# Another static order for the steps of an attention and MoE kernel on one core

## The chip, the cores and the metric

The kernel runs on one NeuronCore of one Trainium2 chip. The metric is the device time of one execution in microseconds. The kernel before took 953.86, 952.43 and 950.26 us in three runs, median 952.43.

## The reference

Attention over a batch of 8, with 8 heads, 576 positions and 64 dimensions, is followed by a root mean square norm and a gated feed-forward layer:

```
scores = scale * q @ k.T                       # [8, 8, 576, 576]
mask_local   = (rel >= 0) & (rel < 32)         # heads 0 to 3
mask_strided = (rel >= 0) & (pos_k % 32 == pos_q % 32)   # heads 4 to 7
attn = exp(scores - max) / (sum + 1e-9)
x = (attn @ v)  as [4608 tokens, 512]
xn = x / sqrt(mean(x * x) + 1e-6) * rms_g
out = (silu(xn @ w_gate) * (xn @ w_val)) @ w_out      # 512 -> 1536 -> 512
```

Everything is float32. Both masks leave at most 32 positions to a query, so only small blocks of the scores are computed.

## The kernel before

**Attention.** There are 32 iterations, one for each batch entry and pair of heads. In each, TensorE multiplies blocks of queries and keys into the PSUM tile `pair` (L288, 72 or 80 small matmuls). VectorE scales and masks them (L308, into the tile `pT` or `pp`) and takes the largest of each row (L311). ScalarE does ten exponentials with sums (L315). VectorE forms the reciprocal of the sums (L319, L320), POOL or VectorE multiplies by it (L322), VectorE transposes (L324). Then TensorE multiplies by the values (L300, in two halves that use the same PSUM tile), and ScalarE (L358) or VectorE (L360) copies each half out into `raw`. Squares (L400, L416, L418) and their sums (L421, tile `ssq`) follow for the norm.

**Norm and feed-forward layer.** The 4608 tokens are nine chunks of 512. For chunk 1, a matmul with ones (L430) sums the squares over the partitions, ScalarE takes the root (L480), VectorE makes reciprocals of it (L483) and scales (L487). Each float32 product is three matmuls of rounded parts, high by high, low by high and high by low: `xh` and `xl` (L501, L516), `hh` and `hl` (L598 or L600, L607), and the two halves of each weight tile. The 1536 inner columns are twelve slices of 128. A slice has g (L540, PSUM tile `g`), v (L540, `v`), the gate (L553 tanh on ScalarE, L555, L591 and L584 on VectorE) and four groups of output matmuls (L616, tiles `acc`). L550 adds a correction to g. Chunk 0 is done in this plain form. Chunks 1 and 2 and later chunks save products by sums of blocks: the sums of the weights are formed by VectorE, POOL and ScalarE (L667, L671, L755, L761), stored in DRAM (`tg`, L769) and loaded again (L777). Chunks 3 to 6 are done in pairs (products at L1593, sums at L1624 and L1643, outputs at L1392), the last two as one pair (L1004). Weights that were moved out come back by DMA (L1246, `wg<-wsg`, `wv<-wsv`). The weights arrive packed and are unpacked by VectorE, ScalarE and POOL in the first part (L1736 to L1758).

**What sets the order.** The program first records 3612 steps, each with the engines that may do it, and issues none. The table `ORDER`, text of compressed bytes, then says for each place which of the steps still left comes next and on which of its engines (`Plan.order`, L143):

```
code = zlib.decompress(base64.b85decode(ORDER))
left, out = list(range(n)), []
for k in range(n):
    i = left.pop(code[k] + 256 * code[n + k])
    out.append(self.ops[i][0][ENGINES[code[2 * n + k]]][2])
```

The steps are issued in that order (L1837 to L1839), each engine keeps its own part of it, and waits between engines follow from the data and the reuse of tiles. Nothing is reordered later: a step that waits holds all that stand behind it on its engine. SP's queue holds the DMA issues in the same manner.

Of the kernel before, what the change touches and what calls it, by code (L numbers as in the profile page):

```python
# [20 lines left out]
NB, NH, S, D = 8, 8, 576, 64  # L21
DM, DF = 512, 1536
# [3 lines left out]
P = 128  # L26
KC = DM // P
# [29 lines left out]

ENGINES = ("PE", "DVE", "ACT", "Pool", "SP")
ORDER = (
    "c-rk)*OMH_dG9o#dve^J4Y#+uw|jeg8MvHr;2i=90z@K600v2bVni$^!ID4_06`KAkSt23#9&g1v?$BvDqD6*a@p3KQ@LDz@W0_FKj_6h-7|Y&`PmPyy1BiX*`DsNzy5"  # L60
    "u{@7Ld~AL)UiXr^Oo8bAc&$1uj4rny+NHRUDs@C!!{tCugcOFmQ2JM?~A(f2C*73HL&>&}ykb4)QFIbxh%dB}M5sAU_<11HS;*)c<b`wqB!k9hj#^nUXD@!ezpg*JY#j"
    "^YUej|?xElNQ6%tvNcxaA#+GP<QLYxVDV{qh|O06P~mGUFo<}sNHYc&6;z>w9P|9R<-}PR`OR?sraiMzu1xdyt&(IH2%)&>;LVK`hH#e*{6R^`aY?C{0|@hec>bWw;wi"
    "t)BME`{^sY+4^}>J?*8RZ<Mlsp#((zG7hlGo|LIu#)6e^V^3hL>=`W4X9-r4f-mlN%AD5@~Pd{lTANe0P*M8uPdmn#)?4zakzlU!j^!^Qew>4qC6Ww_`vff+{t#22t_u"
    "hWjzw`DVqV^jfhI?QCz;eIewBB!DxBh7H+TFzu?oQk9IAP(~IVZjwIPac&?3p{)&yKzkIuD+?{hD`cz`3#ft>t}QG5p46zqc6&2d+fH3+opzAM*C0^9P<q&pdJIig)qS"
    "9`F45<>%w2C!SyTo{hZc=EJj3Cg+yU&OY||;;eW2^r3TKJGF4&@h4Qbc4qQ)_Y~@jE<5$%XOCYPKK4{=*OQ?;Jm!Y0?&<qGr@Ch!?JPbKtj1?nrcd`xo%Bw$qK6-8MfD"
    "?%qtOvRG5W`g2W$I_2m1E?<KDi#d-tri@X>0s_)vdsSJ5r3EG0{e@q({bc6+1I=&~12E`$>c-Dqq&o-PhXlkGwjkKT>nYb4$Ju4E;-y_DQqyg7U0vm3L?$Jb|Go%vysB"
    "!BFet^)6sA_{`&?dVSY*2(zs+i`H>ruFb^?)B@zzrI?&Rt~;-xD+I>Kbzc4E*?nSYghb|o_Ob9DLUbcaag<(6~fpHLigE<>vIS_FZRPTqOJHyP&ncG$J}J`uv@q}A3fR"
    "^MHRPj#E;#A?~O$6xD}Y2gH1NH-e@>hX?ZzXau%Hv3&DKFIa;1^$|cXVCmh?dsd-;$?AW!-n44T-Y{^}`<1SdvoafA#&Xi;C9GRS4wucwGCDxfqSg}?#s_Vv>!B$2>)?"
# [36 lines left out]

# [1794 lines left out]
```

## Time and profile before

| | before |
|---|---|
| median of three runs | 952.43 us |
| profiled execution, its own time | 952.13 us |
| its span | 950.0 us |
| mean granted clock of TensorE | 0.977 |
| TensorE (PE), matmuls | 911.8 us busy, 96%, 8708 |
| VectorE (DVE) | 746.8 us, 79% |
| ScalarE (ACT) | 460.2 us, 48% |
| GpSimd (POOL) | 250.1 us, 26% |
| DMA | 220.76 MB, 232 GB/s |

All times are of the one profiled execution, from the start of its span. A row of a timeline gives the start of an instruction or of a few alike, their length, engine and line, the output and input tiles and, in brackets, how long the engine had stood idle before and what ended that. "issue" there means that the profile shows nothing the engine waited for. The granted clock is a share of TensorE's full clock.

### The profile page before, as it was taken

How to read it: one execution, taken by the hardware profiler on the slowest of the kernel's cores; microseconds unless marked ns; L12 is line 12 of the kernel's file. 1: busy time of each engine (PE TensorE's matmuls, PEld its weight loads, DVE VectorE, ACT ScalarE, POOL GpSimd, SP SyncE). 2: the span in 40 equal slices, each digit the busy share in tenths (PEclk: the TensorE clock that was granted, in tenths of full speed). 3: DMA queues.
4: the chain of work that ended last, by engine and by line, in shares of the span. 5: the costliest groups of instructions: out<-in, count | busy, mean ns of one | idle time of the engine just before them, and what ended most of it. 6: DMA issues, size and time to landing. Idle time of an engine off the chain costs nothing.

```text
span 950.0 us, 21761 instructions
## 1 busy us (share of the span) xinstructions
PE 911.8 (96%) x8708; PEld 734.8 (77%) x8708; DVE 746.8 (79%) x1235; ACT 460.2 (48%) x1308; POOL 250.1 (26%) x213
## 2 busy tenths in 40 slices
PE   4899996999999999999999999999999999999998
PEld 3677774787887877886888887888887878888886
DVE  6889997978788899887669999653679896447883
ACT  7779754445333556544444485342336623224330
POOL 2222233233433521444214313200051320014211
PEclk6799997999999999999999999999999999999999
DMA  9865677684666697874763697755655795576462
GB/s 331 320 255 206 202 254 242 242 293 149 233 214 231 223 290 262 304 279 189 255 221 129 212 306 242 294 210 178 246 204 162 223 352 202 204 269 233 122 223 87
DMA packets 95092, 220.76 MB, mean 232 GB/s; under 512 B 9616, under 2 KB 28688, under 8 KB 94992
## 3 DMA queue, kind: packets, MB, share of 16 engines
q1 hardware_dynamic: 94560, 218.83, 66.4%
q8 instruction: 68, 1.11, 0.5%
q10 hardware_dynamic: 432, 0.56, 0.2%
q14 instruction: 32, 0.26, 0.1%
HBM read 172.17 MB, written 47.19 MB: 231 GB/s over the span
## 4 chain that ended last, share of the span: by engine, by line
PE 77%; DVE 10%; DMA 6%; ACT 3%; issue 2%; SPq 1%; DVEq 0%; ACTq 0%
PE acc L1593 10%; PE acc L540 7%; PE v L1593 7%; PE g L1593 6%; PE acc L1392 6%; PE g L540 5%; PE v L1392 4%; PE v L540 4%; PE g L1392 4%; PE v L1004 3%; PE acc L1004 3%; PE g L1004 3%; PE pair L288 2%; DMA wg<-wsg 2%; PE pair L300 2%
## 5 line engine op out<-in xcount | busy, mean ns | idle before, releaser
L540 PE MATMUL g<-xh,wg 128*128 128x512 f32 x184 | 60.3, 410 | 2.8 <-DVE e L555 2.0
L315 ACT ACTIVATE pT<-pT,mx 128x64 f32<-128x64 f32 x160 | 53.4, 336 | 18.5 <-DVE mx L311 18.5
L540 PE MATMUL v<-xh,wv 128*128 128x512 f32 x184 | 57.9, 396 | 0.5 <-DVE or L584 0.5
L315 ACT ACTIVATE pp<-pp,mx 128x64 f32<-128x64 f32 x160 | 53.4, 338 | 10.1 <-DVE mx L311 10.0
L288 PEld LDWEIGHTS pair<-xx,xx 64*32 64x32 f32 (+1 forms) x2432 | 28.0, 109 | 24.8 <-issue 16.0
L288 PE MATMUL pair<-xx,xx 64*32 64x64 f32 (+1 forms) x2432 | 34.3, 234 | 12.6 <-issue 7.2
L540 PEld LDWEIGHTS g<-xh,wg 128*128 128x128 f32 x184 | 35.7, 198 | 13.0 <-DVE e L555 2.9
L540 PEld LDWEIGHTS v<-xh,wv 128*128 128x128 f32 x184 | 33.6, 188 | 7.8 <-DVE or L584 0.6
L540 PE MATMUL g<-xl,wg 128*128 128x512 f32 x92 | 37.1, 403 | 0.0
L358 ACT COPY raw<-pair 128x128 f32<-128x128 f32 (+8 forms) x64 | 20.9, 373 | 32.8 <-PE pair L300 32.7
L671 POOL TENSOR_TENSOR tt<-tt 128x256 f32<-128x256 f32 (+1 forms) x26 | 24.2, 937 | 46.2 <-DVE tt L671 29.2
L540 PE MATMUL v<-xl,wv 128*128 128x512 f32 x92 | 35.9, 391 | 0.0
L540 PE MATMUL acc<-xh,wg 128*128 128x512 f32 x104 | 33.9, 408 | 0.0
L540 PE MATMUL acc<-xh,wv 128*128 128x512 f32 x104 | 33.4, 404 | 0.0
L616 PE MATMUL acc<-or,hh 128*128 128x512 f32 x96 | 30.7, 398 | 0.8 <-DVE or L1758 0.8
L315 ACT ACTIVATION_READ_ACCUMULATOR pp<-pp,mx 128x1 f32 x160 | 30.4, 190 | 0.0
L315 ACT ACTIVATION_READ_ACCUMULATOR pT<-pT,mx 128x1 f32 x160 | 30.1, 188 | 0.0
L553 ACT ACTIVATE e<-g 128x512 f32<-128x512 f32 x23 | 13.7, 598 | 32.6 <-PE g L540 20.0
L1611 ACT ACTIVATE or<-g 128x512 f32<-128x512 f32 x24 | 14.3, 596 | 31.3 <-PE g L1593 27.2
L1593 PE MATMUL acc<-wg,wv 128*128 128x512 f32 x102 | 29.2, 394 | 0.0
L1593 PE MATMUL acc<-wv,wv 128*128 128x512 f32 x102 | 28.7, 390 | 0.0
L1648 POOL TENSOR_TENSOR wv<-or,or 128x512 f32<-128x512 f32 x2 | 2.6, 1291 | 95.6 <-DVE or L1624 95.6
(854 smaller groups left out, 2920.9 us busy)
## 6 DMA issues: line engine op xcount, KB each, us to landing
wv<-wsv SPq DMA_DIRECT2D x36, 512.0 KB, 6.9
wg<-wsg SPq DMA_DIRECT2D x26, 512.0 KB, 7.5
or<-tg SPq DMA_DIRECT2D x22, 512.0 KB, 5.5
th<-tg SPq DMA_DIRECT2D x21, 512.0 KB, 5.9
tl<-tg SPq DMA_DIRECT2D x21, 512.0 KB, 6.0
xx<-in_qT_dram SPq DMA_DIRECT2D x32, 288.0 KB, 5.4
xx<-in_kT_dram SPq DMA_DIRECT2D x31, 288.0 KB, 5.3
wg<-wos SPq DMA_DIRECT2D x32, 256.0 KB, 5.2
```

The source lines that it names most:

```text
L288: nc.tensor.matmul(out=pair_[32 * y:32 * y + m, h, 64 * g:64 * g + 64], lhsT=q[r, PAD + a:PAD + a + m], rhs=k[r, a:a + 64], start=True, st ...
L300: nc.tensor.matmul(out=dst[z // 2][64 * h:64 * h + 64, z % 2, 320 + c:320 + f], lhsT=v[r, 6 * h + j], rhs=t[r, a:a + f - c], start=j == fi ...
L315: nc.scalar.activation(out=tv[:, g], in_=tv[:, g], func=AF.Exp, bias=m[:, g:g + 1], accum_out=z[:, g:g + 1])
L358: nc.scalar.copy(out=d, in_=s)
L540: nc.tensor.matmul(out=out, lhsT=wt[:, w, sl], rhs=xhl[x, kc], start=(n == 0 and i == 0), stop=(n == KC - 1 and i == 2))
L553: op("ACT", act(CH, True), 0, lambda: nc.scalar.activation(out=e(), in_=out, func=AF.Tanh, scale=0.5), reads=[bk], writes=[ek], tab="exp")
L616: nc.tensor.matmul(out=acc[t], lhsT=x[h][:, sl], rhs=wt[:, w], start=(u == 0 and i == 0), stop=(u == NU - 1 and i == 2))
L671: elementwise(width, lambda e: both(e).tensor_tensor(out=dst(), in0=a(), in1=b(), op=ALU.subtract), [], keys)
L1004: nc.tensor.matmul(out=banks[bk], lhsT=w, rhs=X[a, k].tile(y), start=start and k == 0 and i == 0, stop=stop and k == 1 and i == 2, skip_gr ...
L1392: nc.tensor.matmul(out=banks[bks[j]], lhsT=w.tile(v, k, j), rhs=x.tile(k, y), start=start and n == 0 and i == 0, stop=stop and n == KT - 1 ...
L1593: nc.tensor.matmul(out=banks[bk], lhsT=w, rhs=xtile(a, k, y), start=start and k == 0 and i == 0, stop=stop and k == 1 and i == 2, skip_gro ...
L1611: op("ACT", act(CH, True), 0, lambda: nc.scalar.activation(out=temp(dst), in_=banks[bk], func=AF.Copy, scale=scale), reads=bank_keys(bk), ...
```

## The change

The kernel's steps, their number and what each may run on are the same. Only the table `ORDER` is another, and it is one source line longer, so that every line of the changed kernel behind it has a number one higher than in the kernel before. One line of the 48 and its like:

```diff
 ORDER = (
-    "c-rk)*OMH_dG9o#dve^J4Y#+uw|jeg8MvHr;2i=90z@K600v2bVni$^!ID4_06`KAkSt23#9&g1v?$BvDqD6*a@p3KQ@LDz@W0_FKj_6h-7|Y&`PmPyy1BiX*`DsNzy5"
+    "c-rk)*>fDnd7nP#zILuXXD{q777OCO2m%B_kRU*c6iMjdO@fqY5)7?_vTQ37C0nu%$C50`vJ#a;>ONvwNja`c;#BN%Ra}+#yre2m`3q8c$wQvf(>=4G-t&?wG<GqVp6;"
...
```

The steps of the five engines before and after, as counted from the two tables:

| | TensorE | VectorE | ScalarE | POOL | SP |
|---|---|---|---|---|---|
| before | 1007 | 1180 | 646 | 209 | 570 |
| after | 1007 | 1163 | 656 | 216 | 570 |

In the rows below, the number behind a tile's name and the underscore is a serial number; `pT1`, `hl0` and the like are the tiles, and x12 counts matmuls in a row.

TensorE, about 142 to 155 us of the trace before. Above, from left to right of the flow, stand the last products of v, the two halves of the values product (L300) of one attention iteration, the scores (L288) of a later one, and the sum of squares of chunk 1 (L430). In the kernel before:

```order
L540 MATMUL v_68<-xh1_780,wv10_1506 128x512 x2
L540 MATMUL v_68<-xl1_786,wv10_1506 128x512
L540 MATMUL v_68<-xh3_790,wv10_1506 128x512 x2
L540 MATMUL v_68<-xl3_797,wv10_1506 128x512
L300 MATMUL pair_72<-pT1_98,vt1_86 64x64 x12
L300 MATMUL pair_72<-pT1_98,vt1_86 64x48 x4
L300 MATMUL pair_72<-pT1_98,vt1_86 64x16 x4
L300 MATMUL pair_72<-pT1_98,vt1_86 64x64 x12
L300 MATMUL pair_72<-pT1_98,vt1_86 64x48 x4
L300 MATMUL pair_72<-pT1_98,vt1_86 64x16 x4
L288 MATMUL pair_72<-xx2_82,xx1_81 32x64 x36
L430 MATMUL g_67<-ssq_101,ones_64 128x512
L540 MATMUL g_67<-xh0_442,wg10_1520 128x512 x2
```

And the same part of the changed kernel:

```order
L301 MATMUL pair_72<-pT1_98,vt1_86 64x64 x12
L301 MATMUL pair_72<-pT1_98,vt1_86 64x48 x4
L301 MATMUL pair_72<-pT1_98,vt1_86 64x16 x4
L541 MATMUL v_68<-xh1_690,wv10_1475 128x512 x2
L541 MATMUL v_68<-xl1_772,wv10_1475 128x512
L301 MATMUL pair_72<-pT1_98,vt1_86 64x64 x12
L301 MATMUL pair_72<-pT1_98,vt1_86 64x48 x4
L301 MATMUL pair_72<-pT1_98,vt1_86 64x16 x4
L541 MATMUL v_68<-xh3_762,wv10_1475 128x512 x2
L541 MATMUL v_68<-xl3_777,wv10_1475 128x512
L289 MATMUL pair_72<-xx2_82,xx1_81 32x64 x36
L431 MATMUL g_67<-ssq_101,ones_64 128x512
L289 MATMUL pair_72<-xx0_80,xx3_83 32x64 x32
```

One group of v now stands between the two halves of L300 and one between the second half and L288; behind L430 come the scores of the next iteration, where g stood.

VectorE in the same stretch, from the masking of that iteration's scores (L308, into `pT1`) to their transposition (L324). In the kernel before:

```order
L308 SCALAR_TENSOR_TENSOR pT1_98<-pair_72,cb_63 128x640
L311 TENSOR_REDUCE mx1_74<-pT1_98 128x10
L671 TENSOR_TENSOR tt_105<-tt_105 128x256 x2
L755 CAST th0_1792<-tt_105 128x512
L761 TENSOR_TENSOR tl0_1796<-tt_105,th0_1792 128x512
L755 CAST th0_1792<-tt_105 128x512
L761 TENSOR_TENSOR tl0_1796<-tt_105,th0_1792 128x512
L319 TENSOR_SCALAR mx1_74<-su1_76 128x10
L320 RECIPROCAL mx1_74<-mx1_74 128x10
L322 TENSOR_TENSOR pT1_98<-pT1_98,mx1_74 128x640
L324 STREAM_TRANSPOSE pT1_98<-pT1_98 128x640
```

And in the changed kernel:

```order
L309 SCALAR_TENSOR_TENSOR pT1_98<-pair_72,cb_63 128x640
L312 TENSOR_REDUCE mx1_74<-pT1_98 128x10
L556 SCALAR_TENSOR_TENSOR e_100<-e_100,g_67 128x512
L592 SCALAR_TENSOR_TENSOR e_100<-e_100,v_68 128x512
L601 CAST hh0_103<-e_100 128x512
L608 TENSOR_TENSOR hl0_882<-e_100,hh0_103 128x512
L1752 SCALAR_TENSOR_TENSOR th0_106<-or1_1551 128x512
L320 TENSOR_SCALAR mx1_74<-su1_76 128x10
L321 RECIPROCAL mx1_74<-mx1_74 128x10
L323 TENSOR_TENSOR pT1_98<-pT1_98,mx1_74 128x640
L325 STREAM_TRANSPOSE pT1_98<-pT1_98 128x640
```

The weight sums (L671, L755, L761) have left the place between L311 and L319, and the gate and its rounding (L555, L591, L600, L607) stand there.

VectorE at about 431 to 438 us, in the first pair of chunks that is done together: `wv9` and `wv10` are weight tiles that come back by DMA, `or` takes a sum that TensorE needs. In the kernel before:

```order
L1617 TENSOR_TENSOR acc3_71<-acc3_71,e_4810 128x512
L667 TENSOR_TENSOR hl0_4891<-wv10_5076 128x512
L308 SCALAR_TENSOR_TENSOR pT0_97<-pair_72,cb_63 128x640
L311 TENSOR_REDUCE mx0_73<-pT0_97 128x10
L1624 SCALAR_TENSOR_TENSOR or2_4784<-or2_4784,g_67 128x512
L671 TENSOR_TENSOR hl0_4891<-hl0_4891 128x256
L319 TENSOR_SCALAR mx1_74<-su1_76 128x10
L320 RECIPROCAL mx1_74<-mx1_74 128x10
L1624 SCALAR_TENSOR_TENSOR or4_4840<-or4_4840,acc3_71 128x512
```

And in the changed kernel:

```order
L1618 TENSOR_TENSOR acc2_70<-acc2_70,or2_4806 128x512
L668 TENSOR_TENSOR hl0_4872<-wv9_4558 128x512
L672 TENSOR_TENSOR hh0_4883<-hl0_4872,hh0_4883 128x512
L672 TENSOR_TENSOR hl0_4872<-hl0_4872 128x256
L672 TENSOR_TENSOR hl0_4872<-hl0_4872,hh0_4883 128x256
L309 SCALAR_TENSOR_TENSOR pT0_97<-pair_72,cb_63 128x640
L312 TENSOR_REDUCE mx0_73<-pT0_97 128x10
L1625 SCALAR_TENSOR_TENSOR or3_4828<-or3_4828,acc2_70 128x512
```

The L667 that reads `wv10` has left VectorE for POOL, and one that reads `wv9` stands a few places ahead of L308.

## Rows read from the trace of the kernel before

**Rows 1.** Stretches: from:to, us, busy PE PEld DVE ACT POOL, clock, DMA, GB/s
```profile
0.00:50.00 50.00, 32.79 (x778) 25.44 (x779) 37.51 (x74) 37.13 (x127) 11.37 (x24) 0.70 0.88 330
50.00:134.00 84.00, 82.44 (x735) 65.44 (x733) 79.29 (x127) 67.25 (x162) 22.85 (x16) 1.00 0.68 236
134.00:165.00 31.00, 21.80 (x373) 15.76 (x363) 23.62 (x39) 14.08 (x53) 11.27 (x11) 0.78 0.60 199
165.00:340.00 175.00, 172.16 (x1951) 139.00 (x1950) 146.52 (x242) 78.46 (x266) 63.05 (x53) 1.00 0.66 230
...
766.00:950.00 184.00, 179.23 (x787) 147.02 (x785) 120.05 (x198) 52.52 (x93) 26.90 (x20) 1.00 0.59 208
```

**Rows 2.** Page: busy time by engine; a DMA queue (packets, MB, share)
```profile
PE 911.8 (96%) x8708; PEld 734.8 (77%) x8708; DVE 746.8 (79%) x1235; ACT 460.2 (48%) x1308; POOL 250.1 (26%) x213
...
q8 instruction: 68, 1.11, 0.5%
```

**Rows 3.** TensorE's timeline, 134 to 165 us: start, length, instruction, [idle <-releaser]
```profile
134.66 1.02 PE L288 MATMUL pair<-xx,xx 64*32 64x64 f32 x80 [0.55 <-ACT raw L358]
...
137.32 0.50 PE L616 MATMUL acc<-or,hl 128*128 128x512 f32 x1 [0.98 <-DVE hl L607]
...
139.04 0.62 PE L616 MATMUL acc<-or,hh 128*128 128x512 f32 x2
...
139.72 0.62 PE L540 MATMUL v<-xh,wv 128*128 128x512 f32 x2
...
144.67 1.00 PE L300 MATMUL pair<-pT,vt 32*64 32x64 f32 x40 [2.06 <-DVE pT L324]
...
148.47 1.08 PE L288 MATMUL pair<-xx,xx 64*32 64x64 f32 x52 [0.78 <-ACT raw L358]
151.66 0.64 PE L288 MATMUL pair<-xx,xx 64*32 64x64 f32 x20 [2.11 <-issue]
...
155.08 1.22 PE L540 MATMUL g<-xh,wg 128*128 128x512 f32 x2 [0.78 <-ACT srt L480]
...
156.53 1.05 PE L540 MATMUL g<-xh,wg 128*128 128x512 f32 x2
...
157.81 1.05 PE L540 MATMUL g<-xh,wg 128*128 128x512 f32 x2
```

**Rows 4.** VectorE's timeline, 130 to 180 us
```profile
135.50 1.77 DVE L607 TENSOR_TENSOR hl<-e,hh 128x512 fp32r<-128x512 f32 x1
...
142.35 0.17 DVE L319 TENSOR_SCALAR mx<-su 128x10 f32<-128x10 f32 x1 [0.51 <-ACT pT L315]
...
143.67 0.84 DVE L324 STREAM_TRANSPOSE pT<-pT 128x640 f32<-128x640 f32 x1
...
165.92 0.68 DVE L607 TENSOR_TENSOR hl<-e,hh 128x512 fp32r<-128x512 f32 x1
...
175.92 1.20 DVE L319 TENSOR_SCALAR mx<-su 128x10 f32<-128x10 f32 x1
```

**Rows 5.** POOL's timeline, 130 to 180 us
```profile
135.21 1.51 POOL L1758 TENSOR_TENSOR or<-th,or 128x512 fp32r<-128x512 f32 x1 [3.29 <-ACT or L1756]
...
175.79 1.29 POOL L667 TENSOR_TENSOR tt<-wv 128x512 f32<-128x512 f32 x1
```

**Rows 6.** TensorE's timeline of the opening
```profile
15.05 0.44 PE L288 MATMUL pair<-xx,xx 64*32 64x64 f32 x7 [2.80 <-issue]
```

**Rows 7.** TensorE's timeline around 307 us
```profile
307.58 0.50 PE L540 MATMUL acc<-xl,wv 128*128 128x512 f32 x1 [0.70 <-issue]
```

**Rows 8.** VectorE's timeline around 434 us
```profile
433.72 0.69 DVE L667 TENSOR_TENSOR hl<-wv 128x512 f32<-128x512 f32 x1 [1.61 <-DMA wv<-wsv]
```

**Rows 9.** TensorE's timeline around 437 us
```profile
436.65 0.96 PE L1593 MATMUL g<-wg,wg 128*128 128x512 f32 x3 [1.16 <-DVE or L1624]
...
438.96 0.96 PE L1593 MATMUL acc<-wg,or 128*128 128x512 f32 x3 [0.66 <-DVE or L1624]
```

**Rows 10.** TensorE's timeline where the last pair of chunks begins
```profile
773.99 1.63 PE L1004 MATMUL g<-raw,wg 128*128 128x512 f32 x6 [0.98 <-DMA wg<-wsg]
```

More of the change, by code (lines that the diff above doesn't have):

```diff
@@ new lines @@
+    ")|<M;i(Z-89i%*isgv8)ma(M^Pr1QpqVvL!$8w7l_@d`o{)&S_Y+EwV+{WwQDxA<9|BK22m|8W^6mG^`-19zWuqRoAI=7_C|(WR$L;)%`X^OK|mn_AW{Ke*(o_QvTbep"
+    "fdkoRvF;fGV)+gzBgJn^V7r8znSe=9}NqpRT$b+H1$qk6zygi<$miF^uLRP-&Ovp5&gOz=}Xn{uVX#<YWVBw??3-t^jZ9mCG_#%7eD%A>7R=q4E*74`1?CXBmWf~s6}7"
+    "C_j%R-`qSa~Z+c&S?SJ_d{Nk^=Uv)qGq5?np1h#+qE3frSuW;vFVf@pN3m?M|-zt6--Pv_FxAfug`{XYl?veMPy+ORUXOF*Sy%E1|HQ#x6_3d{mZ~fq>-`nfHKD7UCP@"
+    "Dh7t2KA{&wcm3oB8uM^0x=ye87J5bS|`CyD|X$AC;f9Px!C;_N%wgymbFdFP=s($K{uf<Q{r9eDImj+E^=CPx%{99fXg62L$W>V~;N1eB}D%wcOH^k3C^M9$HtXgB#Yh"
@@ new lines @@
+    "r5oScTDrRX#;J4Pau%*^E;yGi4mjtpHqTAD-j&UXP48mi!dT&)+xT|==84?!mUn%{+vtvUgTc$*@Md)6e6+GYG`AT&JaFm4z=cjcefG@s>8R1E)E}rkI6QD-{lp=Ec<5"
+    "*?t{*Pf4j(@BFKe|!>;77}u^8@OsMMF2Dof49%4#*7Z^d)frMMB-N6O*u>IaRxv)#sY<Ne8A<Gu0mcgI&6W6Q1m<&}D~zEr5!_7rL#6=$l?m*eNke=$*c=9&0P{LbaK<"
+    "M7h+w{ZC5QmN6%7f)@~tU`SI)OTa&nacP5@^{PeccKa{8pWuPFWrc?2BSg{MnMz?`JkLH6{GyATEOl%!qUkTN5bIPnPB;6!M-Ti$S<A<gZsm3GdL0i>-nKlaIn~k+J)9"
+    "q=jh%}cX6R}XiujQY=xcWMz{om=0Xt92aR2oN<NsJjDqoFVSX$e*&VDYemghS8VtsPZ;#A--f%IPE_jnK=b~}h9gTu^*mH-5+-@-IcKlA;t(M$kuIv^o6}w!>H)FeAA!"
@@ new lines @@
+    "e!KkCe+!X{g`~792Cm=R)(4RW-e)HCVP<?m!qf+`3hBs+Mil>*f94V99f2Gb%XNtP#djwrLq-=Co}Y4P$)FG^!osR?uMC(TjG`F4)C<C10`ilBIi^=IXw7)9z?JN9$^X"
+    "ksg}Wi&wSS(8@Vo>ps+VhBdpbSp!B(8_<r`o6W}I0ne@0t1r2W?!+rKGB&5pub1LO>g;+^T`8ysj8Sd*di$E%>dm)QbwHVJH_rtV4P2A&yHAegU2>%>kFbl@8j`!({K0"
+    "tz&s%fUsLi7)iYH?-?vzJIX3KaQPnGb*_#_@<Kcjer{p`Z{A9|Q{0fJQsTa_AYRI9L>FXhW{vT%0-j#JouPY&Mgcs<zd5;*-^=uG~{Y^(m8fiXDR9fALD$L)UwL!b;gA"
+    "2i#bR0MOkK%-U%G3Zp<Z&Fa|{h8eEwl_hiRnC=2!$o=b!3ep>az*%5!FSiZo38(M&h2!54u>9jc?jkP9ROPAC*~&V+Gx!%M`9PKLu#1`Ujy-<#5cgxg?%yz!cq{)c@Rv"
@@ new lines @@
+    "{TycUH?%$xq4u>4ObJRX=udW|$k#*=FTs~;7cxDb8i^gIdSo)m4jvgvc>JWNhH3#;&d!Ji10JVUo%Er8^lk3yYEZI`6a!DO6kpdnhrxnr-N^qzs7ch;EVjWlZ9ayq77#"
+    "hBhbj6cHXHvCanVwax7uBipx5^{>^Sh8&FSNbm-Fy#4Ik_nx_7(fkN^F<#b+sTX6cGZ7#)bmHDHqHTTXywbj((5~$)J6301Ph5V6(Aj&RJ;H2%f|ys*-V{?;;uk3S5=l"
+    "+^<}Cl@5Oq0_#&B#2!H986Cht_2JJIC_6IzDJ5hW;U2+**u=&UG1TVkv)WAMS*`qi9pZxO|7}t66h+a?iq|ZnPEJ?!5Xxm$@v%$;Onk#7map52>1d8^SQgPEo!lncvxL"
+    "fo(x=TL9j9ZF{uBww6aLn(ed4LgZ?@<)gHmwGK<Hv!lhG##X&46x#VF?!myn!I{MU%-yi5#IGZ)Qx&vRrzBkK3^24zN254ey9@Fu#B?Ja|$Q#Gz^UN$coT2)oyFUnAc1"
@@ L103 @@
+    "oP8B$7HPbp(yPMP-<QemM$9Lko8j1sWqd?6trG3#qmXT!9jrObx<ZMn#cEWMInkkbQiVK{t525wg_0l5sFJnxx&m|`)*5J>wWNjyv2fHW5YpOn&024|p669uMN78IERR"
+    "*-R;HiASsVtGbjo>PME)9wz4R~Ug1u}r+%h)yx>8naE=OAE|+ljjYBqRUESj#BCt4oI>$Yb&6X@kvT2+YQ7$kmGItHj+R_Uj6PCZ^I#toFq)Xr^QU8npFbfxU79a+bW1"
+    "lri{=|;vvEP|LG?=&XpIF%=!3#0p=m_O#"
 )
```

66 lines of the change are left out of this document (24 added, 42 removed).

## The prediction

> **What bounds the kernel now.** I read the table of stretches first [rows 1]. TensorE is busy in 911.8 of 950.0 us [rows 2], and the reader is to see where the missing 38.2 us lie: 17.2 in the first 50 us, 1.6 from 50 to 134, 9.2 from 134 to 165, 2.8 to 340, 4.8 in the last 184, and the 2.6 that are left from 340 to 766. No other engine has so much work: VectorE stands highest from 50 to 134, with 79.29 of 84 us. So the same instructions in another order can win the idle time of TensorE and no more, apart from the clock: the granted clock is 1.00 in every stretch but two, 0.70 in the first and 0.78 in the third. [...] A triple of 128x512 matmuls takes 0.68 us from start to start at the upper level (139.04 to 139.72) and 1.28 at the lower (156.53 to 157.81) [rows 3].
>
> The second view is TensorE's timeline from 134 to 165 [rows 3], the third VectorE's there [rows 4]. The reader is to see one chain: VectorE's L607 takes 1.77 us at 135.50 instead of the 0.68 of the same line at 165.92 while POOL works on L1758 [rows 4, 5]; TensorE waits 0.98 us for it; the softmax behind it on VectorE starts late, and the values product L300 waits 2.06 us for the transposition L324, the next scores L288 wait 0.78 for a copy out of PSUM, then 2.11 for nothing that the profile shows ("issue"), and the g matmuls wait 0.78 for the root L480. Together 5.73 us of holes that follow one another, after a first one of 0.98.
>
> The fourth view is the waits on "issue". In the opening there are four, the first of 2.80 us [rows 6]. Counted over TensorE's matmuls, weight loads and semaphore rows from the start, the instruction at which TensorE resumes is number 449, 705, 961 and 1473 of them, then 3521 at 151.66 and 7105 at 307.58 [rows 3, 7]: each 256 apart or a multiple of it. The page's queue of instructions moves 68 packets of 1.11 MB together, 16.3 KB each, for 17416 matmuls and weight loads, 256 for a packet [rows 2]. I read this so: TensorE's instructions come in pieces of 256, and a piece of dense small matmuls (L288, L300) is used up before the next has come. A piece can only be made longer in time by what else stands in it.
>
> **The change part by part.** The 3612 steps stay; TensorE's stand 3.3 places away from before on average, 381 steps change their engine (123 from VectorE to POOL, 116 back, 75 from VectorE to ScalarE, 65 back, 2 between ScalarE and POOL).
>
> *134 to 165 us.* The scores before that wait of 2.06 us (L288 at 134.66) now stand four to five groups earlier, and behind them stand ten triples of 0.68 us instead of eight before L300 needs the transposition: 6.8 us of cover for 5.4. Before, the chain from the end of the scores (134.66 + 1.02 = 135.68) to that of the transposition (143.67 + 0.84 = 144.51) took 8.8 us, of which the first 1.5 was VectorE still busy with L607, to 137.27. Without that it is 7.3, so of the 2.06 about 0.5 stays: -1.5. If VectorE is as late as before, it is 8.8 - 6.8 = 2.0 and nothing is won; if it is earlier, -2.06. One triple now stands between the two halves of L300 and one between L300 and L288: 0.68 us each against the wait for a copy, 0.78 at 148.47 and as much, near enough, between the two halves: -1.3. The piece border still lies in the same L288, but its piece now holds those triples, two more less one that left: the TensorE work in it (its instructions in the new order, by their spacing before) rises from 2.8 to 4.0 us, and the 2.11 falls by the same 1.2 to 0.9: -1.2. L430 has a full L288 of 80 matmuls behind it where g stood: about 1.0 us, more than the 0.78 wait for the root: -0.8. The 0.98 for L607 goes too, but its steps are mixed with others in the new order, and I count 0.2 of it. Sum -5.0, bounds 0 and -8 (all the holes named, and the clock held: 3 triples at 1.28 instead of 0.68 are 1.8 more).
>
> *307.58 us.* The piece whose end stalled 0.70 us held 5.2 us of work, counted in the same way, and now holds 9.2: -0.7, bounds 0 and -0.7.
>
> *433 to 439 us.* VectorE stands at L667 until a weight load lands (idle 1.61), behind it wait L308, L311 and L1624, and TensorE waits 1.16 and 0.66 us for two L1624 [rows 8, 9]. The load is now 12 places earlier in SP's queue, and that L667 is on POOL, so that VectorE's queue no longer waits with it: -1.8. Bounds 0 (another L667, with an earlier load, now stands a little ahead of the same place) and -1.8.
>
> *First 50 us.* Border stalls of the same kind stay: the first pieces hold 1.6, 1.6, 1.6, 3.7 and 3.8 us of TensorE's work where they held 1.6, 1.6, 2.5, 4.4 and 3.5. A four-copy evacuation moves from ScalarE and one L1758 from POOL to VectorE. I take 0; bounds -2.8 and +2.8 (one stall as the first of [rows 6] less or more).
>
> *The rest.* What is idle elsewhere is 1.6 + 2.1 + 1.2 us (50 to 134; 165 to 340 without 307.58; the last stretch without what lies behind its last matmul), and 0.8 of the 2.6 later. The largest is the 0.98 at 773.99, for a weight load [rows 10]. The pair that begins there now needs two loads at its first product, queued one behind the other at once: between none and twice the 0.98, I take it as unchanged. Of the others I count 1.5 as gone. Against it stand new ones: in an order in which TensorE's steps move by three places, waits of the size of those there now come up elsewhere, above all from 50 to 134, where VectorE has 4.7 us to spare; I take +2.5, bounds 0 and +5.
>
> Sum: -5.0 - 0.7 - 1.8 + 0 - 1.5 + 2.5 = -6.5 us. From the profiled execution's 952.13 that is 945.6; the median of the runs is 952.43, 0.3 above it, so 945.9 for what will be timed.
>
> **The rivals.**
>
> *The gain of 134 to 165 is eaten by VectorE and POOL.* For it: beside POOL's instructions VectorE's own take longer. L319, 0.17 us at 142.35 with POOL idle, took 1.20 at 175.92 while POOL had L667, and L607 its 1.77 beside L1758 [rows 4, 5]: 1.0 and 1.1 us too long. The change gives POOL seven steps more, and puts four L671 and one L1758 on POOL just there. Four such collisions at 1.0 us in the chain L607, L319, L322 and the sums of squares behind it are 4 us: -2.5 in all instead of -6.5, thus 949.9. Against it: VectorE's column shrinks by 17 steps, at 0.6 us (746.8 / 1235) some 10 us. [...]
>
> *It does not do what it says.* The borders fall in stretches as dense as before, and the stall at 151.66 stays whole because the next piece is asked for when the former border is passed and the holes in front of it, in which it came nearer, are gone. Then the 2.06 and the copies are won only to be waited for at the border: -1 instead of -5, and the sum is -2.5 + 1.0 (a new stall in the opening's pieces) = -1.5: 950.9. For it speaks that the opening's short pieces are no longer in time than before; against it, that the piece in question has become longer.
>
> [...]
>
> **How the numbers follow.** Less than 0.5% (4.8 us) is not told from no change here. The forecast has 0.60, its own range 941.5 to 949.5, and 0.52 of it is under 947.7. VectorE and POOL 0.14, the borders 0.10: both no change. The opening 0.16, of which 0.12 over 957.2 and 0.04 within. So faster 0.52, no change 0.08 + 0.14 + 0.10 + 0.04 = 0.36, slower 0.12. The range, 940.5 to 955.5, takes in the first two rivals and the better part of the third, and below the forecast the bounds of the third stretch with the clock.
>
> **What would show it.** In the profile after: the granted clock from 134 to 165 and idle time there under 5 us; no wait of L300 for L324 over 1 us near 140; a wait on "issue" of about 1 us in the scores ahead of L430; none near 307; none for L1624 near 436; 17 us idle in the first 50. The prediction is wrong if the third stretch is still idle for 8 us, or if waits of TensorE for VectorE between 50 and 134 sum to over 5 us; a granted clock under 0.68 in the first 50 us would show the third rival.

## The result and the profile after

The changed kernel took 936.70 us (median of four runs, 935.01 to 938.68) where the kernel before took 951.86 in the same comparison: a ratio of 0.984, 95% interval 0.981 to 0.987. It is 15.2 us faster. The forecast of 945.9 had the direction and less than half of the size, and the time lies below the range's lower end of 940.5. The profiled execution of the changed kernel took 938.68 us, with a span of 936.9.

The table of stretches of the changed kernel, with the columns of [rows 1]:

```profile
0.00:50.00 50.00, 36.52 (x800) 29.00 (x801) 37.71 (x79) 38.27 (x126) 11.82 (x24) 0.73 0.80 289
50.00:134.00 84.00, 80.34 (x797) 63.24 (x796) 81.52 (x127) 68.99 (x177) 23.00 (x18) 1.00 0.64 222
134.00:165.00 31.00, 26.78 (x323) 20.54 (x322) 27.23 (x45) 15.73 (x40) 6.98 (x6) 0.94 0.71 253
...
766.00:936.90 170.90, 166.68 (x733) 136.80 (x731) 112.62 (x180) 44.07 (x80) 30.75 (x23) 1.00 0.57 198
```

The reader is to see the first row and the third. TensorE is idle for 13.5 us of the first 50, where it was 17.2, and for 4.2 of the 31 from 134 on, where it was 9.2; the clock of that stretch rose from 0.78 to 0.94. From 50 to 134 the idle time grew, 1.6 to 3.7 us, while VectorE's work there went from 79.29 to 81.52.

By what ended them, the waits of TensorE of 0.15 us or more add up so: on "issue" 12.5 us before and 5.0 after, for ScalarE 5.2 and 1.3, for VectorE 15.7 and 15.6, for transfers 1.4 and 3.7. That is 9.2 us less waiting; the matmuls themselves are busy for 4.3 us less (911.8 to 907.5). The largest single gain lies in the waits on "issue", of which the forecast had counted 1.9 (1.2 and 0.7).

TensorE's timeline of the changed kernel, which answers to [rows 3]:

```profile
137.79 0.77 PE L301 MATMUL pair<-pT,vt 32*64 32x64 f32 x40
...
140.99 1.01 PE L289 MATMUL pair<-xx,xx 64*32 64x64 f32 x72
142.69 1.12 PE L431 MATMUL g<-ssq,ones 128*128 128x512 f32 x2 [0.70 <-DVE ssq L422]
143.75 1.02 PE L289 MATMUL pair<-xx,xx 64*32 64x64 f32 x80
...
151.20 1.20 PE L541 MATMUL g<-xh,wg 128*128 128x512 f32 x2 [3.48 <-DVE e L556]
...
152.63 1.05 PE L541 MATMUL g<-xh,wg 128*128 128x512 f32 x2
...
153.91 0.98 PE L541 MATMUL g<-xh,wg 128*128 128x512 f32 x2
```

The waits for the transposition (2.06), for the two copies, for the root and, against the forecast, all of the wait on "issue" (2.11) are gone: the 72 scores at 140.99 run through. The sum of squares L431 starts at 142.69; in the kernel before it came at 152.23. Then a new wait of 3.48 us comes, and behind it the triples stand 1.28 us apart (152.63 to 153.91): the clock fell only here, to a share of 0.50 from 151.3 to 154.6 us. The new wait's chain, on VectorE and on POOL:

```profile
149.66 0.88 DVE L672 TENSOR_TENSOR tt<-tt 128x256 f32<-128x256 f32 x2 [1.20 <-POOL tt L808]
150.46 0.68 DVE L556 SCALAR_TENSOR_TENSOR e<-e,g 128x512 f32<-128x512 f32 x1
```

```profile
148.37 1.26 POOL L808 TENSOR_TENSOR tt<-tt,or 128x512 f32<-128x512 f32 x1 [10.40 <-DMA or<-wos]
```

L556, which frees the tile `g`, stood on VectorE behind a sum L672 whose other half POOL could only form when a weight had landed. VectorE stood idle for 1.20 of the 3.48 us; in the rest it had other work. No wait over 0.15 us is left at the places of [rows 7, 9, 10].

**Where the 13.1 us of the two profiled spans came from.** I laid the two traces beside each other by TensorE's steps: after the same amount of its work, how far is the changed kernel ahead? (Each step counts with the shorter of its two spacings, without waits.) This distance is called the lead below. The forecast gave its new waits (-2.5) and the rest (+1.5) for the whole kernel; here they stand at one stretch each. The column on the right is a second profiled execution of the changed kernel (after_again, below).

| stretch, by the time before | forecast | measured | again |
|---|---|---|---|
| 0 to 51 | 0 | +4.1 | +5.4 |
| 51 to 130 | -2.5 (new waits) | -1.9 | -2.8 |
| 130 to 167 | +5.0 | +7.3 | +10.2 |
| 167 to 339 | +0.7 (307.58) | +0.1 | +1.2 |
| 339 to 465 | +1.8 (L1624) | +3.2 | +2.6 |
| 465 to 525 | 0 | -2.1 | -2.1 |
| 525 to the end | +1.5 (all the rest) | +2.4 | +2.4 |
| sum | +6.5 | +13.1 | +16.9 |

### The profile page after: what moved, and what is told of

Read it like the earlier page. It is cut to its first block, busy times and chain, and to the rows that moved or that the text cites. A ratio compares the mean times of both kernels' runs of the same rounds, so it can differ in the third digit from the quotient of the medians.

```text
span 936.9 us, 21775 instructions
## 1 busy us (share of the span) xinstructions
PE 907.5 (97%) x8708; PEld 733.7 (78%) x8708; DVE 758.8 (81%) x1224; ACT 464.9 (50%) x1312; POOL 263.0 (28%) x220
## 3 DMA queue, kind: packets, MB, share of 16 engines
q8 instruction: 68, 1.11, 0.5%
## 4 chain that ended last, share of the span: by engine, by line
PE 66%; DVE 10%; DMA 2%; issue 1%; ACT 1%; POOL 1%; SPq 0%; DVEq 0%; ACTq 0%; POOLq 0%
PE acc L1594 10%; PE acc L1393 7%; PE v L1594 6%; PE g L1594 6%; PE g L1393 5%; PE v L1393 5%; PE g L1005 3%; PE v L1005 3%; PE acc L1005 3%; PE acc L541 3%; PE v L541 2%; PE v L1170 2%; PE g L1170 2%; PE pair L289 2%; PE acc L1170 2%; PE g L541 2%
## 5 line engine op out<-in xcount | busy, mean ns | idle before, releaser
L541 PEld LDWEIGHTS g<-xh,wg 128*128 128x128 f32 x184 | 35.4, 198 | 16.3 <-DVE e L556 8.8
L289 PEld LDWEIGHTS pair<-xx,xx 64*32 64x32 f32 (+1 forms) x2432 | 28.0, 109 | 19.4 <-issue 12.0
L672 POOL TENSOR_TENSOR tt<-tt 128x256 f32<-128x256 f32 (+1 forms) x25 | 20.8, 840 | 48.6 <-DVE tt L672 28.4
L301 PEld LDWEIGHTS pair<-pp,vt 32*64 32x64 f32 x784 | 18.1, 139 | 8.8 <-issue 6.2
```

Of the source, the lines that this page charges most:

```text
L289: nc.tensor.matmul(out=pair_[32 * y:32 * y + m, h, 64 * g:64 * g + 64], lhsT=q[r, PAD + a:PAD + a + m], rhs=k[r, a:a + 64], start=True, st ...
L301: nc.tensor.matmul(out=dst[z // 2][64 * h:64 * h + 64, z % 2, 320 + c:320 + f], lhsT=v[r, 6 * h + j], rhs=t[r, a:a + f - c], start=j == fi ...
L541: nc.tensor.matmul(out=out, lhsT=wt[:, w, sl], rhs=xhl[x, kc], start=(n == 0 and i == 0), stop=(n == KC - 1 and i == 2))
L672: elementwise(width, lambda e: both(e).tensor_tensor(out=dst(), in0=a(), in1=b(), op=ALU.subtract), [], keys)
```

## The experiments

All ratios are to the kernel before, run in the same comparison. Line numbers are those of the kernel before, except in after_again and e_order.

**One part of the order alone.** A splice takes the first steps from one order, each with its engine there, and the steps that are left in the other. The seam is the place where the two meet.

h_open has the changed opening, h_a130 the changed order up to about 130 us:

```diff
-order = before
+order = after[:200] + rest of before      # h_open
+order = after[:573] + rest of before      # h_a130
```

> The first 200 steps (some 50 us) in the changed order, the rest in the order of before. If the opening is worth what the two traces show at its end (TensorE 4.1 us further on for the same work), the time falls by 4, to 948. If VectorE's backlog from 50 to 134 us takes it back, as the prediction's value of 0 would have it, it stays within 1 of 951.9. TensorE's idle time in the first 50 us should be 13 to 14 us in either case, against 17.2.

> The changed order to 130 us, before's after that. In h_open TensorE's lead of 4.5 us at 51 us was lost again by 62 us. If what keeps it in the changed kernel is the engine moves and order of 50 to 130 us, the lead is still 2 to 3 us at 125 us here, and 1 to 3 us of it reach the end: 949 to 951. If it is lost at any seam, it is 952 or more.

h_open: 0.9978 (0.9958 to 0.9997); h_a130: 0.9987 (0.9965 to 1.001). The opening's gain is there in both: after the work that the kernel before had done at 51 us they lead by 4.5 and 3.8 us. h_open then loses it within ten microseconds, at its seam:

```profile
52.03 0.73 PE L540 MATMUL g<-xh,wg 128*128 128x512 f32 x2 [1.28 <-DVE e L555]
56.72 0.70 PE L616 MATMUL acc<-or,hh 128*128 128x512 f32 x2 [1.67 <-DVE hh L600]
58.31 0.50 PE L616 MATMUL acc<-or,hl 128*128 128x512 f32 x1 [0.89 <-DVE hl L607]
```

h_a130, in which the changed order goes on, keeps 2.4 of it at 125 us. So the opening is worth some 4 us on TensorE, of which some 2.4 are left at 125 us; it was counted at nothing. The total of h_a130 is not told apart from that of the kernel before.

h_third has the third stretch alone, h_late all that comes after it:

```diff
-order = before
+order = before[:570] + after[:800] + rest of before   # h_third
+order = before[:800] + rest of after                  # h_late
```

> Before's order up to 130 us, the changed order from there to 190, before's again after that. Theory: the scores ahead of L430 cross their piece border before the wave of transfers starts, so the instructions of the next piece come at once: no wait on issue there, and the whole stretch is worth 7 to 9 us: 943 to 945. The prediction's sizes (a longer piece, 0.9 of the 2.11 us left): 5 us, 947, with a wait on issue of about 1 us.

> Before's order to 185 us, the changed order after that. From the two traces the later places add 2 to 3 us (waits at 437 and 774 us gone, new ones at 499 and 511): 949 to 950. If they are worth nothing without what came earlier: 952.

h_third: 1.0043 (1.0016 to 1.0071); h_late: 1.0074 (1.0048 to 1.0100). Both were expected to be faster (943 to 947, 949 to 950) and are slower, so the total holds what the seam costs and does not tell what the stretch is worth. By TensorE's lead h_third gains 8.6 us over the third stretch (0.9 to 9.5 us at the work that before had done by 160), still leads by 8.7 at 190, and gives it back behind its seam:

```profile
193.76 0.27 PE L300 MATMUL pair<-pp,vt 32*64 32x64 f32 x2 [1.66 <-DMA vt<-in_vs_dram]
197.88 1.22 PE L540 MATMUL acc<-xh,wg 128*128 128x512 f32 x2 [2.12 <-DVE hl L555]
...
210.93 0.73 PE L540 MATMUL g<-xh,wg 128*128 128x512 f32 x2 [1.32 <-DVE e L555]
```

h_late loses 11 us at its seam (a wait of 6.1 us for one L584) and from there wins 3.6 back, as much as the places from 339 on bring in the table above. Splices show what a stretch is worth only if read up to the seam.

**Order and engines apart.** e_order has the changed order with every step on the engine it had before, e_engines the reverse:

```diff
-(step, engine) = after's order, after's engine
+(step, engine) = after's order, before's engine     # e_order
+(step, engine) = before's order, after's engine     # e_engines
```

> The changed order of all 3612 steps, but each on the engine that it had before: none of the 381 moves between engines. If the order of TensorE and of the transfers makes the gain, at least 10 of the 15 us stay: under 942. If the relief of VectorE by the moves makes it, it falls by less than 5: over 947, with waits for VectorE from 50 to 165 us in its place.

> Before's order of all 3612 steps, each on the engine that the changed kernel gives it: the 381 moves alone. If moves and order only work together (the order alone was 4% slower), this is slower as well, by 10 us or more, with new waits of TensorE for VectorE and POOL. If the moves are a relief by themselves, it is up to 5 us faster: 947 to 951.

1.0401 (1.0364 to 1.0437) and 1.0523 (1.0491 to 1.0555): neither half is worth anything alone. TensorE stands idle for 64.5 and 70.8 us of the two spans (38.2 before); its waits for VectorE add up to 44.0 and 38.5 us where they were 15.7. The line of busy times on the page of e_order, then of e_engines:

```profile
PE 924.3 (93%) x8708; PEld 736.9 (75%) x8708; DVE 784.0 (79%) x1235; ACT 460.8 (47%) x1308; POOL 263.6 (27%) x213
```

```profile
PE 925.5 (93%) x8708; PEld 734.8 (74%) x8708; DVE 785.7 (79%) x1224; ACT 464.5 (47%) x1312; POOL 278.0 (28%) x220
```

VectorE is busy for 37 and 39 us more than in [rows 2] with the same or fewer instructions. I counted its instructions that took over 0.1 us longer than the short ones of the same line and operands, and whether POOL was busy meanwhile:

```
            longer beside POOL     longer without POOL
before       45, 26.1 us            8, 2.1 us
after        67, 45.5 us           13, 3.3 us
e_order      82, 59.1 us            6, 1.7 us
e_engines    84, 62.4 us           12, 3.4 us
```

So nearly all of the stretching stands beside POOL, and the two halves double it. How much of their loss it makes is not shown: the changed kernel has 19.4 us more of it than the kernel before and is faster, and e_order has 13.6 us more than the changed kernel and takes 54 us longer. What makes an instruction longer beside POOL is not shown, and not all are: in the kernel before L324 took 0.84 us at 37.20, with POOL at work for all of it, and 0.84 at 143.67 without POOL.

**What the wait on "issue" hangs on.** A border is the place in TensorE's instructions where one piece of 256 ends and the next begins; the instruction queue of the changed kernel moves 68 packets of 16.3 KB for 17416 matmuls and weight loads too, 256 for each. Two kernels take transfers away from the time between the border at 144.91 us in the kernel before and the start of the packet behind it, at 149.25. b_wave moves three stores out of the wave that SP issues from 139.9 us on in the kernel before, ahead of the stalled piece; b_wave2 also moves the steps of VectorE and POOL that overwrite the stored tiles:

```diff
 L805 or<-wos
-L769 tg<-th
-L769 tg<-tl
-L1762 wsv<-wv
 ...
 L262 kT load
+L769 tg<-th        # b_wave: behind a load at 152.7 us
+L769 tg<-tl
+L1762 wsv<-wv
 L555 e<-e,g        # b_wave2: six L755, L761, L667 behind it
```

> Before, with three of SP's seven issues between 139.9 and 145.1 us (two stores to tg, one to wsv, 1.5 MB) moved behind the loads that wait until 152 us. Theory: the fetch of TensorE's next instruction piece, asked for at 144.9 us, stands behind these transfers; with them gone its packet starts by 146.5 instead of 149.25, and the wait on issue of 2.11 us in the scores ahead of L430 is under 0.5: 2 to 4 us faster, 948 to 950. Rival (the piece is too short by its work alone): the wait stays at 2.1 us, and the time within 1 us of before.

> b_wave, and the six steps of VectorE and POOL that overwrite the tiles whose stores were moved (L755, L761, L667) stand behind L555, so that VectorE does not wait for the stores ahead of it. In b_wave the wait on issue was gone and L430 started 3.4 us earlier, but VectorE then waited 4.6 us for a store and g 4.5 us for L555. If that wait alone took the gain back, this is 2 to 4 us faster than before: 948 to 950. If something else holds the g products at 162 us, it stays at 952.

TensorE of b_wave, then its VectorE:

```profile
147.59 1.34 PE L288 MATMUL pair<-xx,xx 64*32 64x64 f32 x72 [0.78 <-ACT raw L358]
148.86 2.07 PE L430 MATMUL g<-ssq,ones 128*128 128x512 f32 x2
...
161.68 1.08 PE L540 MATMUL g<-xh,wg 128*128 128x512 f32 x2 [4.47 <-DVE e L555]
```

```profile
155.66 0.43 DVE L755 CAST th<-tt 128x512 fp32r<-128x512 f32 x1 [4.59 <-DMA tg<-th]
```

The order of TensorE is untouched, its piece of 256 holds the same work, and the wait on "issue" is gone: L430 came 3.4 us earlier than before, of which 1.0 was there at 130 us, ahead of the moved stores. In h_open and h_late, which have the same border as before, the wait was 1.57 and 1.54 us, so it differs between executions, but only b_wave and b_wave2 have none. The total is the same, 1.0006 (0.999 to 1.0023), and not 948 to 950 us as expected, because VectorE now stood at L755 for a tile that the moved store still read, and held L555. b_wave2 takes the wait for L555 down to 1.11 us and meets others (2.18 at 170.30 for one L501): 1.0027 (1.0002 to 1.0052). Gone at one place, the time is paid at the next; but the question of the piece is answered.

j_third and j_open do the reverse to the changed kernel: copies from DRAM to DRAM that serve nothing fill the DMA engines at the moment at which the border is crossed (shares of 0.85 and 0.81, in the table below).

```diff
 recip mx1                                   # about 135 us
+dma jg <- mx1                               # holds the copies until then
+10 x dma jk <- in_kT_dram   (288 KB each)   # j_third
 xh of chunk 0                               # about 30.6 us
+dma jg <- xh
+8 x dma jk <- in_kT_dram    (288 KB each)   # j_open
```

> The changed kernel with ten copies of 288 KB from DRAM to DRAM, of no use to the output, issued from SP when the recip step ahead of the transposition at 136.9 us has ended, that is at about 136 to 140 us. Theory: the packet of TensorE's next piece starts 3 to 4.5 us after the border at 138 instead of 0.8, and the scores ahead of L431 wait 1.5 to 3 us on issue, which they did not do at all. Rival (work in the piece decides): no wait on issue there. Both: SP's loads behind the copies are some 4 us late, which alone may cost as much again in the g products at 151.

> The changed kernel with eight copies of 288 KB of no use from DRAM to DRAM on SP at 30.6 us, where its queues are idle. Theory: the packet of TensorE's instruction piece asked for at 32.3 us starts at 35 to 36.5 us instead of 33.4, and TensorE waits 1 to 2 us on issue at 36 us, where before waited 1.9 and the changed kernel 0; the lead at 40 us falls from 3 by that. Rival (work in the piece): no wait on issue there. Loads behind the copies are 3 us late in both.

TensorE of j_third, then of j_open:

```profile
141.56 0.41 PE L288 MATMUL pair<-xx,xx 64*32 64x64 f32 x18 [0.87 <-issue]
...
155.38 1.22 PE L540 MATMUL g<-xh,wg 128*128 128x512 f32 x2 [8.42 <-DVE e L555]
```

```profile
37.58 0.28 PE L300 MATMUL pair<-pT,vt 32*64 32x16 f32 x1 [1.65 <-issue]
```

Each brought a wait on "issue" back at a border that the changed kernel passes without one. j_open came to 0.9901 (0.9872 to 0.9929), in two runs: beside the changed kernel its lead was 3 us lower behind that place and 3.7 lower at the end. j_third came to 0.9901 (0.9864 to 0.9939), but its stall is only 0.87; most of the loss is the 8.42, since the copies also held back the weight that VectorE needs (it waited 6.47 us for it). The packets came 2.27 and 2.34 us after the border, less than the 3 to 4.5 that were expected.

m_fetch measures the fetch by itself: 2048 small matmuls that serve nothing (two instructions each in the trace, 4096) stand ahead of the kernel before, with 32 copies after the first 1024.

```diff
+dense(1024)                  # matmuls 32x64, in the trace 2048, 107 ns each with their load
+32 x dma jk <- in_kT_dram
+dense(1024)
 kernel before
```

> Before, with 1024 small matmuls (64 rows, 32 by 64, zeros) in front of it while the DMA queues are nearly idle, and 1024 more while 32 copies of 288 KB run: 16 instruction pieces of nothing but small matmuls, 1.6 us of work each at the upper clock. Theory: with idle queues a piece comes 3.0 to 3.8 us after the border before it, with full queues 5 to 7.5. Rival: the same interval in both halves.

One run, 1391.72 us. The DMA records of the instruction queue, beside TensorE's borders (times in us; the DMA share is that of the 2.3 us from 0.3 ahead of the crossing on; "next" is the packet that follows it):

```
kernel     border crossed  next packet starts  DMA share  wait at the next border
before         35.05          3.61 later          1.04      1.86
after          32.29          1.11 later          0.07      none
j_open         31.93          2.34 later          0.81      1.65
before        144.91          4.34 later          0.96      2.11
after         137.98          0.80 later          0.26      none
b_wave        144.02          1.63 later          0.38      none
j_third       136.90          2.27 later          0.85      0.87
m_fetch, 14 pieces with idle queues: 1.6 earlier (mean)     none
m_fetch,  2 pieces with full queues: 0.8 and 1.8 later, share 1.04 to 1.05
```

Where TensorE waited, it went on 2.2 to 2.6 us after the packet's start, in j_open 3.3 us after it (its packet took 1.82 us, those of the kernel before at such places 0.9 to 1.1). In m_fetch the expectation failed: a piece took 13.7 us and not 1.6, so that none stalled, and with idle queues the packets came ahead of the border and not 3.0 to 3.8 us behind it. What it shows is the difference, from two packets: full queues made them 2.4 to 3.4 us later. In the seven other rows the four with a DMA share of 0.81 to 1.04 had the packet 2.27 to 4.34 us after the border and a wait of 0.87 to 2.11 us at the next one; the three with 0.07 to 0.38 had it after 0.80 to 1.63 us and no wait. I read from them that a packet stands behind the data transfers of that moment; no record shows when it is asked for. How long the piece lasts counts too: the two late packets of m_fetch, ahead of pieces of 13.7 us, cost nothing.

**Single places of the changed order.** c_third puts two of the v groups back in front of L300. i_swap, to mend the new waits, puts six steps (L553, L555, L591) ahead of sums and of unpacking steps:

```diff
+L540 v (two groups)      # c_third: ahead of L300
 L300 pair<-pT,vt
-L540 v (two groups)
+L555 e<-e,g              # i_swap: ahead of L671, L1751, L1746
 L671 tt<-tt
```

> The changed kernel with the two v groups that stand between the halves of L300 and ahead of the scores put back in front of L300, where before had them. The prediction's terms for them: waits for a copy of 0.75 and 0.78 us come back (1.4), and the piece's border is met sooner after its fetch was asked for, a wait on issue of 0.5 to 1.5 us. L431 starts 1.5 to 3 us later than in the changed kernel, and by the clock and the wait for L556 behind it 1 to 3 us of that reach the end: 938 to 940. If the wait of 3.5 us behind L431 for L556 hides it, the time stays at 937.

> The changed kernel with five gate steps of VectorE one to three places earlier, ahead of weight steps that stood in front of them: L556 and L592 ahead of the L672 that waits for POOL (g waits 3.5 us there), and L556 at 56.0, 81.6 and 91.8 us ahead of L1752 and L1747 that took 1.7 to 1.8 us beside POOL. By the waits 1.3 + 0.8 + 0.9 + 1.2 us: 933 if all are kept, ratio 0.980. If VectorE's sum and not its order sets those waits, they come back at the next gate: 936 to 937, ratio 0.984.

> The changed kernel again, beside the others on one chip: 936 to 937, ratio 0.984.

> The five gate steps earlier, again, to set it against the changed kernel on the same chip. If the waits that went in its profile (1.3 us at 151, 0.9 at 82, 1.2 at 92) are worth their sum less the new ones (0.9 at 51, 0.6 at 96), it is 2 us faster than the changed kernel; if VectorE's sum sets the pace, it is the same within 0.5.

TensorE of c_third, then the third stretch of after_again and TensorE's wait in it:

```profile
140.61 0.77 PE L300 MATMUL pair<-pT,vt 32*64 32x64 f32 x40 [0.78 <-ACT raw L358]
142.16 0.97 PE L288 MATMUL pair<-xx,xx 64*32 64x64 f32 x72 [0.78 <-ACT raw L358]
143.44 1.12 PE L430 MATMUL g<-ssq,ones 128*128 128x512 f32 x2 [0.31 <-DVE ssq L421]
...
150.68 0.93 PE L540 MATMUL g<-xh,wg 128*128 128x512 f32 x2 [2.17 <-DVE e L555]
```

```profile
134.00:165.00 31.00, 28.02 (x336) 21.69 (x335) 29.73 (x48) 18.09 (x53) 8.36 (x8) 1.00 0.78 280
```

```profile
149.39 0.73 PE L541 MATMUL g<-xh,wg 128*128 128x512 f32 x2 [2.17 <-DVE e L556]
```

c_third came to 0.9856 (0.9825 to 0.9887) beside after_again's 0.9828 (0.9796 to 0.9860): 2.0 us more by the medians, within the intervals. The two waits of 0.78 for a copy that the triples had covered came back, as priced, and no wait on "issue" did, against the expectation: its packet had started at 138.79, 3.9 us ahead of the border at 142.67. The v groups behind L300 pay for the copies and for nothing at the border. after_again is the changed kernel once more, and its clock held at 1.00 behind a wait of 2.17, where it fell behind the 3.48. The length of the wait does not settle this: behind a wait of 2.17 the clock of c_third fell too (0.94 in this stretch). i_swap came to 0.9850 (0.9823 to 0.9876) and once more to 0.9820 (0.9789 to 0.9851); the waits near 82 and 92 us were gone, others of 0.5 to 0.9 came, and it is not told apart from the changed kernel. No version here is shown to beat that one.

## Why the forecast was too small

**The opening was counted at 0; shown for one of its borders.** "Border stalls of the same kind stay" failed: the opening brought 4.1 us (5.4 in after_again). The stalls were priced by the work in the pieces, which changed little. At the borders TensorE waits 2.10, 0.97 and 0.91 us, 4.0 together:

```profile
15.38 0.43 PE L289 MATMUL pair<-xx,xx 64*32 64x64 f32 x6 [2.10 <-issue]
...
21.50 0.93 PE L289 MATMUL pair<-xx,xx 64*32 64x64 f32 x47 [0.97 <-issue]
...
25.79 1.66 PE L406 MATMUL v<-few,ssq 128*128 128x4 f32 x8 [0.91 <-issue]
```

Before there were 2.80 [rows 6], 2.29, 1.77 and 1.86, 8.7 together. The 4.7 of difference cover the lead of 4.1 at 51 us; the other waits up to there grew by 1.0. By the prediction's own count only one of the pieces holds more work than before, the fifth, 3.8 us for 3.5. At the first of these borders the packet was no sooner (3.8 us after the crossing, 3.6 before); there a wait of 1.96 us for a transfer inside the piece had taken its time already. At the other three the packets came 3.9, 1.7 and 1.1 us after the crossing, where it had been 4.9, 3.6 and 3.6. j_open shows the last of them: filled with transfers, the border behind it, at 37.58, waits again. The other traces bear out this one alone. b_wave, b_wave2, h_third and h_late have the opening of before and wait 1.9 to 2.4 us at the fourth border, where after_again, c_third and i_swap, with the changed opening, do not wait. At the first border the four wait 1.4 to 2.9 and these three 1.5 to 2.3, at the second 1.4 to 2.6 and 0.7 to 1.8, so that there as much differs between executions as between the orders. The lead holds: at 51 us it is -0.2 to 1.0 for the four and 4.0 to 5.4 for the three. What makes the part of it that the fourth border does not is open.

**Shown: the border term of the third stretch.** It was worked out as if the packet came as late as before, so that 1.2 more work in the piece took 1.2 off the 2.11. All of it went. In the kernel before SP's wave of seven issues stood between 139.9 and 145.1 and the border was crossed at 144.91 in the midst of its transfers; the changed kernel crosses at 137.98, ahead of all but the first of its own:

```profile
137.78 0.59 SPq L806 DMA_DIRECT2D or<-wos  x1
140.43 2.15 SPq L800 DMA_DIRECT2D tt<-wos  x2
```

b_wave removed the stall by the wave alone. The rival on borders, that the stall stays whole, fell with it; that the next piece is asked for at the border before fits the packets in the table above that start 0.80 to 4.34 us behind it, and not those of m_fetch with idle queues, 1.6 us ahead of it.

**The clock counted at 0.** The waits for the chain (2.06 gone, 1.5 forecast), the copies (1.53 and 1.3), the root (0.78 and 0.8) and L607 (0.98 and 0.2) all went. All holes from 134 to the g groups went from 8.0 to 1.0 us, so 7.0 instead of 5.0. The lead grew by 11.2 up to the same work, so the remaining 4 are steps that ran at the upper level and not at the lower (a share of 1.00 and of 0.50 in both traces; between 134 and 165 us it was 0.50 for 13.7 us before, from 145.8 on, and for 3.4 after, from 151.3 on), which the sum left at nothing and only the bound of -8 had, with 1.8. Behind that, 3.8 us went to the new wait of 3.48 in the profiled run and 0.9 in after_again. That the clock holds because the holes went is argued from these runs; no kernel changed the clock alone, and behind the wait for L556 it fell in some executions and held in others (last section).

**Right.** The L1624 term (1.8; the stretch brought 3.2 and 2.6), and the stall of 307.58, which is gone. Idle time of 4.2 us in the third stretch, under the 5 named, no wait for L324, none near 307 and 436. Wrong among the signs: the wait on "issue" of about 1 us ahead of L430 (none came), and 17 us idle in the first 50 (13.5).

**Right by luck: the new waits.** From 50 to 134 the loss of 1.9 to 2.8 fits the -2.5, and the waits there are all for VectorE. But the -2.5 stood for the whole kernel, with a bound of 5. Beside the 3.2 us of waits from 50 to 134 there came 0.70 and 3.48 (for L422 and L556, above), 0.75 at 253.85, 0.88 at 498.92 and 0.79 at 511.40, 9.8 us together. That is beyond the bound, and the gains, which were put too small, hid it.

**The rivals.** VectorE and POOL do collide more, as the first said: VectorE's time rose by 12.0 us with 17 steps fewer, and the count above has 19.4 us more beside POOL. It did not take the gain: TensorE's waits for VectorE add up to as much as before (15.6 and 15.7 us). Where it did cost is the stretch from 50 to 134. There TensorE waits 0.81, 0.93 and 1.19 us for L556, each time behind an unpacking step of VectorE that took 1.83, 1.80 and 1.73 us beside POOL. Without it the same two lines (L1747, L1752) took 0.63 to 0.74. The first, on VectorE and on POOL:

```profile
53.56 0.68 DVE L1747 SCALAR_TENSOR_TENSOR or<-or 128x512 uint32<-128x512 uint32 x1
54.28 1.83 DVE L1752 SCALAR_TENSOR_TENSOR th<-or 128x512 uint32<-128x512 uint32 x1
```

```profile
54.27 1.30 POOL L1759 TENSOR_TENSOR wg<-tt,wg 128x512 fp32r<-128x512 f32 x1 [2.75 <-ACT wg L1757]
```

The opening did not get slower: no run shows the loss for which the 0.12 over 957.2 stands. TensorE was 4.1 us ahead at 51 us, and the clock of the first 50 us was 0.73 where it had been 0.70.

**Open.** Why the two halves of the change lose 39 and 48 us is not settled, and how much of the timed 15.2 us is the clock cannot be said, since it differs between executions.

## What to carry to other kernels

In the table of borders, outside m_fetch, four were crossed with the DMA engines busy (shares of 0.81 to 1.04) and TensorE waited 0.87 to 2.11 us at the next; three were crossed at 0.07 to 0.38 and it did not wait. The length of the piece alone did not price these stalls. Look at the transfers around that moment and move them or the border. Read a spliced order by TensorE's lead up to the seam, since the total holds the seam's own waits. An order and a choice of engines that were found together are one change: taken apart, each was 4 to 5% slower here.

## What the runs showed that I had not expected

The granted clock behind the same wait is not the same in every execution. i_swap and i_swap_again are one kernel, and both wait 2.14 us for L555, at 148.62 and at 148.94. Their stretch from 134 us on, i_swap first:

```profile
134.00:165.00 31.00, 28.09 (x328) 21.61 (x328) 29.03 (x46) 16.71 (x45) 7.65 (x7) 0.94 0.79 280
```

```profile
134.00:165.00 31.00, 27.94 (x333) 20.92 (x332) 29.20 (x47) 17.15 (x47) 8.11 (x7) 1.00 0.79 283
```

Behind that wait the triples stand 1.28 us apart in the first (150.54 to 151.82) and 0.69 in the second (150.45 to 151.14).

A share of the clock has to be set beside the lengths of the matmuls. In the first 50 us, i_swap_again, then j_third:

```profile
0.00:50.00 50.00, 36.35 (x799) 28.81 (x800) 37.62 (x79) 37.86 (x126) 11.81 (x24) 0.93 0.79 286
```

```profile
0.00:50.00 50.00, 36.50 (x805) 28.76 (x806) 38.63 (x81) 39.06 (x133) 12.70 (x25) 0.97 0.79 288
```

The changed kernel has 0.73 there. But the same 72 scores take as long in all three, the changed kernel first, then i_swap_again and j_third:

```profile
27.38 1.34 PE L289 MATMUL pair<-xx,xx 64*32 64x64 f32 x72
```

```profile
27.96 1.34 PE L288 MATMUL pair<-xx,xx 64*32 64x64 f32 x72
```

```profile
27.81 1.34 PE L288 MATMUL pair<-xx,xx 64*32 64x64 f32 x72
```

The share around the first of them is 0.50 (26 to 30 us); at 1.00 (140 to 142 us) 72 scores took 1.01 us in the changed kernel. The profiles of i_swap_again and j_third hold no record of the clock ahead of 32 us, and the share takes such time as full. So 0.93 and 0.97 do not show a higher clock, and what a higher clock would bring in the opening stays open: of its first 50 us the kernel before has 30.5 on record at a share of 0.50 (9.3 to 33.2, and from 43.4 on) and the changed kernel 27.3 (11.3 to 31.8 and 38.6 to 45.4), and no run here shows all of the opening at 1.00.
